# A fused attention, expert and feed-forward kernel: the low halves of expert weights made by an adding DMA instead of GpSimd, and score products over all 128 rows

## The chip, the cores and the metric

The kernel runs on one core of a Trainium2 chip. The metric is the device time of one execution in microseconds (us), the median of three runs. The engines are TensorE (PE; PEld is its weight load), VectorE (DVE), ScalarE (ACT), GpSimd (POOL) and SyncE (SP, which here only issues DMAs).

## The reference

Three blocks follow each other. Only the shapes and the arithmetic matter:

```python
# attention: B, H, S, D = 4, 8, 576, 64
scores = np.where(causal, -1e9, q @ k.T / sqrt(D)); a = exp(scores - max); a /= a.sum(-1) + 1e-9
local = a @ v
mem_out = (phi(q) @ M_prev) / (phi(q) @ z_prev + 1e-6)          # phi(x) = elu(x) + 1
x = g * mem_out + (1 - g) * local                               # g = sigmoid(beta), per head
# experts: N, D, E, F = 2304, 512, 8, 1024; capacity N // E = 288
logits = x @ w_gate        # all (token, expert) pairs by falling logit; a pair is taken
                           # if the token is free and the expert has room
out[mask_e] = maximum(x[mask_e] @ w1[e], 0) @ w2[e]
# second network: d_ff = 2048, w_in and w_out arrive as float64
h = x @ w_in; g = h * tanh(softplus(h)); return g @ w_out
```

## The kernel before, in words

**Precision.** Every fp32 product that counts is made of three fp32r products. A number is held as a high part (rounded to fp32r) and a low part, low = x - high, and the sum takes high x high, low x high and high x low. `mm3` (L998) does this for the networks.

**Attention** has 16 units (a batch and a pair of heads), each in six steps of 128 or 64 query rows: step 4 once for each head ((4,0) and (4,1)), then 2, 1, 0 and 3. A step passes four stages. `stage_a` (L277) makes the scores in PSUM: L298 multiplies 128 rows that hold the high and low q of a head (64 + 64), L304 the low part of k with the high q, 64 rows, one head in the upper and the other in the lower half of the array, and L309 adds the causal mask as a matmul. `stage_b` (L332) transposes the probabilities, `stage_c` (L351 to L359) multiplies them with v and phi(q) with the memory, `stage_d` (L382) finishes. SP loads each unit's q and k, splits them into `q1`, `k1` and `kl` by SBUF transfers (q<-qh, q<-ql, k<-kh), and then issues the loads of the next unit (`ahead`). The last step of the list uses forms of 64 rows or columns where only 64 queries remain.

**The converter** (L745) turns the float64 weights of the second network into fp32 bit by bit on VectorE, with a ScalarE step and, on GpSimd, a product (L783) and a sum (L785). 16 conversions run beside the attention; 16 more are started by `conversions()` (L1088) once four experts are known.

**Experts.** The router works out one expert's tokens after another by a search in thresholds (`phase` L566, `search` L686): VectorE compares (L695, L702), TensorE counts (L707, L722), and they alternate. Each expert has 288 tokens, fetched by three indirect DMAs from GpSimd's queue (L973), transposed on TensorE (L984) and split. Its weights come as 16 tiles `raw` of 128x512 fp32 (L913, on SP; four buffers); for each, ScalarE rounds the high part (L932) and GpSimd subtracts (L942) for the low part, into one of seven `wf` buffers. Once all routing is done VectorE subtracts instead. The second network's first half (resident wa, wb) is woven into the experts, with its gate on ScalarE and VectorE (L1065 to L1081); its second half comes after the experts.

**What sets the order.** TensorE's and GpSimd's orders are written out by a hand planner that hands out slots of six matmuls to generators (`spawn`, `until`); a GpSimd instruction keeps the place it was given. VectorE, ScalarE and SP are ordered by the scheduler from the same program. The dictionary `X` (L1224) holds the planner's settings: LD is the lead, in slots, between a weight's load and its split, RAWB, WFB and ACTB are buffer counts.

Of the kernel before, what the change touches and what calls it, by code (L numbers as in the profile page):

```python
# [33 lines left out]
def attention(tc, ctx, q, k, v, M_prev, z_prev, beta, w_gate, xd, L, side=None):  # L34
# [68 lines left out]

    VZ = []
# [62 lines left out]
    def prep(u, piece):  # L167
# [22 lines left out]
        else:  # L190
# [15 lines left out]
            else:  # L206
# [5 lines left out]
                p["last"] = dq.dma_start(q1[bb, 1], f(p["qh"][bb]))  # L212
# [11 lines left out]
    def prep_first():  # L224
# [26 lines left out]
        for h, s in enumerate(halves):  # L251
# [5 lines left out]
            nc.scalar.copy(r(q1[:, h, 64:S]), tq[h])  # L257
            nc.vector.tensor_sub(r(q1[o, h, 0:64]), zq[o, h], q1[o, h, 0:64])
# [18 lines left out]
    def stage_a(u, i):  # L277
# [17 lines left out]
        kb = (SK - w, 0)  # L295
        for h in heads:
            for a, e in cuts:
                nc.tensor.matmul(vw[h][0:n, a:e], q1[:, h, c0:w], k1[:, h, kb[h] + a:kb[h] + e], start=True,  # L298
                                 stop=False, skip_group_check=True)

        for a, e in cuts:
            for h in heads:
                s = halves[h]
                nc.tensor.matmul(vw[h][0:n, a:e], q1[s, h, c0:w], p["kl"][s, kb[h] + a:kb[h] + e], start=False,  # L304
                                 stop=True, skip_group_check=True)
        for h in heads:

            dg = w - n if h else 0
            nc.tensor.matmul(vw[h][0:n, dg:dg + n], identb[0:n, 0:n], cmask[0:n, 0:n], start=False, stop=True,  # L309
                             skip_group_check=True)  # L310
        if hs is None:
            nc.vector.tensor_reduce(nm[0:n, :], sb[0:n, :, 0:w], axis=AX.X, op=OP.max, negate=True)
        else:
            nc.vector.tensor_reduce(nm[0:n, hs:hs + 1], vw[hs][0:n, 0:w], axis=AX.X, op=OP.max, negate=True)  # L314
        for h in heads:
            nc.scalar.activation(P[0:n, h * w:(h + 1) * w], vw[h][0:n, 0:w], AF.Exp, bias=nm[0:n, h:h + 1], scale=1.0,  # L316
                                 accum_out=den[0:n, h:h + 1])
# [3 lines left out]
    def stage_b(u, i):  # L321
# [7 lines left out]
        for m, eng in GROUPS[i if hs is None else (i, hs)]:  # L329
            t = bank("pt", "pt", 2)  # L330
            for j in range(m):
                nc.tensor.transpose(t[:, j * 128:j * 128 + n], P[0:n, (c + j) * 128:(c + j + 1) * 128],  # L332
                                    ident[0:n, 0:n])
            (nc.scalar.copy if eng else nc.vector.tensor_copy)(  # L334
                T[:, c:c + m, 0:n], t[:, 0:m * 128].rearrange("p (a b) -> p a b", b=128)[:, :, 0:n])
            c += m

    def stage_c(u, i):
# [11 lines left out]
        om = o[0:n, 128 + 2 * W:130 + 4 * W]  # L350
        nc.tensor.matmul(om, p["phi"][:, c0:w], MZ[b % 2][:, hp], start=True,  # L351
# [3 lines left out]
        nc.tensor.matmul(o[:, 0:n], ZB[b]["v"][:, hp, :], T[:, i, 0:n], start=True, stop=(i == 0),  # L355
# [6 lines left out]
        (nc.scalar.copy if i in OTA else nc.vector.tensor_copy)(st["oT"][:, 0:n], o[:, 0:n])  # L362
        nc.vector.tensor_scalar(den[0:n, 2:4], om[:, 2 * W:], 1e-6, None, op0=OP.add)
# [3 lines left out]
    def stage_d(u, i):  # L367
# [14 lines left out]
        nc.tensor.matmul(o[0:n, 128:128 + 2 * W], st["oT"][:, 0:n], R[:, hp].rearrange("p h w -> p (h w)"), start=True,  # L382
# [362 lines left out]
def converter(tc, w_in, w_out):  # L745
# [7 lines left out]
    def convert(a, f, cv, raw, parts=None):  # L753
# [44 lines left out]
def moe(tc, ctx, C, xd, L, w1, w2, w32, whl, convert, out):  # L798
# [19 lines left out]
    eng = [nc.gpsimd, nc.vector]  # L818
# [104 lines left out]

    def splits():
        for c, n, key in order:
# [38 lines left out]
    turned = [-1]  # L964
    xts = {}

    def tokens(k):

        while R.done <= k or turned[0] < k - 1:
# [315 lines left out]
```

## Time and profile before

| | us |
|---|---|
| median of 3 runs (lowest to highest) | 1160.05 (1156.46 to 1165.70) |
| the profiled execution | 1158.69 |
| its span, first to last instruction | 1156.9 |
| mean granted TensorE clock | 0.943 |
| TensorE busy | 1031.9 (89%) |
| VectorE busy | 718.1 (62%) |
| ScalarE busy | 635.5 (55%) |
| GpSimd busy | 407.1 (35%) |

In time the program has a start of some 20 us, the attention to about 300 us, a short stretch in which only the first routing runs (to about 340 us), the experts with the routing of the next ones beside them (to about 820 us), and then the last experts and the second network without routing. A clock of 1.00 is 2.4 GHz; 0.50 is 1.2 GHz, and numbers between them are means over time at both. Most rows below give a start or a stretch in us from the first instruction. An instruction's duration in the trace includes the time in which it has begun and is held up by something that the trace doesn't name.

### The profile page before, as it was taken

The page shows a single profiled execution, that of the slowest core. Times are in us where ns is not written, and L with a number is a line of the kernel's source. Part 1 is how long each engine was busy: PE and PEld are TensorE (multiplying, and loading weights), DVE is VectorE, ACT ScalarE, POOL GpSimd, SP SyncE. Part 2 cuts the span into 40 slices and gives each one's busy share as a digit, 9 for nine tenths or more (in the row PEclk, how much of TensorE's full clock was granted, in tenths as well). Part 3 has the DMA queues.
Part 4 walks back from the last instruction along what each step waited for, and adds up shares of the span by engine and source line. Part 5 has one row for each costly group of instructions (what it writes and reads, how often), then busy time and mean ns, then how long its engine had stood idle before and what let it go on. Part 6 is the DMA issues. An engine that isn't in the chain of part 4 may idle for free.

```text
span 1156.9 us, 22179 instructions
## 1 busy us (share of the span) xinstructions
PE 1031.9 (89%) x8088; PEld 928.7 (80%) x8088; DVE 718.1 (62%) x1954; ACT 635.5 (55%) x1539; POOL 407.1 (35%) x466
## 2 busy tenths in 40 slices
PE   5999999999826969788988879899999999999996
PEld 4777777777625968777877768798999999999996
DVE  7788787865565566658676777768544453333442
ACT  5676676766403443433533443545765786667773
POOL 4676575653207144315325345523200001111112
PEclk9999999999957979889889989989999999999999
DMA  7799689663195232303514422527362532222201
GB/s 179 196 228 234 179 210 230 180 176 82 42 345 149 82 90 91 121 20 107 168 53 134 142 76 96 179 68 248 123 221 75 191 126 83 83 82 83 73 21 41
DMA packets 165628, 153.46 MB, mean 133 GB/s; under 512 B 88912, under 2 KB 134000, under 8 KB 163472
## 3 DMA queue, kind: packets, MB, share of 16 engines
q1 hardware_dynamic: 162272, 142.45, 42.7%
q0 software_dynamic: 3248, 9.61, 2.9%
q8 instruction: 63, 1.03, 0.4%
q14 instruction: 45, 0.37, 0.1%
HBM read 97.17 MB, written 36.18 MB: 115 GB/s over the span
## 4 chain that ended last, share of the span: by engine, by line
PE 67%; DVE 17%; ACT 7%; DMA 4%; issue 2%; POOL 2%; SPq 0%; POOLq 0%; ACTq 0%; DVEq 0%
PE h L1000 20%; PE acc L1000 19%; PE o L359 4%; PE pt L332 4%; PE s L298 3%; PE s L304 3%; PE o L351 2%; PE o L382 2%; DVE H L1078 2%; PE rt L707 2%; DVE cm L702 2%; PE o L355 2%; PE s L309 1%; ACT L1074 1%; PE tr L195 1%
## 5 line engine op out<-in xcount | busy, mean ns | idle before, releaser
L1000 PE MATMUL acc<-act,wb 128*128 128x288 f32 x1536 | 235.5, 304 | 6.2 <-DVE act L1081 2.6
L1000 PEld LDWEIGHTS acc<-act,wb 128*128 128x128 f32 x1536 | 216.8, 193 | 9.1 <-DVE act L1081 3.8
L942 POOL TENSOR_TENSOR wf<-raw,wf 128x512 fp32r<-128x512 f32 x93 | 128.3, 1393 | 239.3 <-ACT wf L932 192.4
L1078 DVE TENSOR_TENSOR H<-H,U 128x288 f32<-128x288 f32 x128 | 68.7, 547 | 177.6 <-ACT U L1074 177.6
L1000 PE MATMUL h<-xt,wf 128*128 128x288 f32 x768 | 126.9, 313 | 3.8 <-DVE xt L993 2.8
L1166 POOL DMA_INDIRECT out<-xg,idx x24 | 25.9, 1077 | 288.3 <-ACT xg L1163 287.0
L1000 PE MATMUL h<-y,wa 128*128 128x288 f32 x768 | 119.7, 311 | 3.4 <-DVE y L993 2.5
L1000 PEld LDWEIGHTS h<-xt,wf 128*128 128x128 f32 x768 | 112.7, 200 | 11.0 <-issue 8.8
L1000 PE MATMUL acc<-act,wf 128*128 128x288 f32 x768 | 120.1, 307 | 0.0
L1000 PEld LDWEIGHTS h<-y,wa 128*128 128x128 f32 x768 | 110.5, 199 | 6.6 <-DVE y L993 3.0
L1000 PE MATMUL h<-xt,wa 128*128 128x288 f32 x768 | 113.2, 296 | 0.0
L932 ACT CAST wf<-raw 128x512 fp32r<-128x512 f32 x128 | 78.8, 617 | 62.1 <-PE acc L1000 20.6
L1000 PEld LDWEIGHTS acc<-act,wf 128*128 128x128 f32 x768 | 108.5, 194 | 4.8 <-issue 4.3
L1000 PEld LDWEIGHTS h<-xt,wa 128*128 128x128 f32 x768 | 105.2, 188 | 0.0
L1065 ACT ACTIVATE U<-h 128x288 f32<-128x288 f32 x128 | 53.2, 416 | 93.0 <-PE h L1000 92.6
L1041 ACT ACTIVATE act<-h 128x288 fp32r<-128x288 f32 x64 | 26.2, 410 | 136.9 <-PE h L1000 136.8
L334 ACT COPY T<-pt 128x512 f32<-128x512 f32 (+4 forms) x128 | 56.8, 446 | 78.7 <-PE pt L332 78.5
L316 ACT ACTIVATE P<-s,nm 128x576 f32<-128x576 f32 (+4 forms) x160 | 83.7, 531 | 6.5 <-DVE nm L314 4.5
L332 PE MATMUL pt<-ident,P 128*128 128x128 f32 (+1 forms) x400 | 68.8, 280 | 0.0
L388 POOL TENSOR_TENSOR xa<-y 128x144 f32<-128x144 f32 (+1 forms) x80 | 47.9, 599 | 44.4 <-DVE y L386 24.2
L707 PEld LDWEIGHTS <-cm 128*32 128x32 bf16 (+1 forms) x756 | 26.2, 107 | 43.7 <-DVE cm L702 30.2
L359 PE MATMUL o<-T,vm 128*64 128x128 f32 x640 | 60.9, 287 | 0.0
(230 smaller groups left out, 2026.8 us busy)
## 6 DMA issues: line engine op xcount, KB each, us to landing
raw<-moe_w SPq DMA_DIRECT2D x128, 256.0 KB, 3.0
k<-kh SPq DMA_DIRECT2D x60, 160.0 KB, 2.9
yd<-y SPq DMA_DIRECT2D x8, 1152.0 KB, 5.3
xt<-yd SPq DMA_DIRECT2D x8, 1152.0 KB, 5.9
raw<-moe_w_in SPq DMA_DIRECT2D x16, 512.0 KB, 4.6
raw<-moe_w_out SPq DMA_DIRECT2D x16, 512.0 KB, 4.5
whl<-parts SPq DMA_DIRECT2D x16, 512.0 KB, 4.5
part<-o SPq DMA_DIRECT2D x8, 576.0 KB, 3.4
```

Source lines behind the costliest of these rows:

```text
L298: nc.tensor.matmul(vw[h][0:n, a:e], q1[:, h, c0:w], k1[:, h, kb[h] + a:kb[h] + e], start=True, stop=False, skip_group_check=True)
L316: nc.scalar.activation(P[0:n, h * w:(h + 1) * w], vw[h][0:n, 0:w], AF.Exp, bias=nm[0:n, h:h + 1], scale=1.0, accum_out=den[0:n, h:h + 1])
L332: nc.tensor.transpose(t[:, j * 128:j * 128 + n], P[0:n, (c + j) * 128:(c + j + 1) * 128], ident[0:n, 0:n])
L334: (nc.scalar.copy if eng else nc.vector.tensor_copy)(T[:, c:c + m, 0:n], t[:, 0:m * 128].rearrange("p (a b) -> p a b", b=128)[:, :, 0:n])
L359: nc.tensor.matmul(o[s, 0:n], vm[:, j - 1 if h else 4 - j, h, :], T[:, i + j if h else i - j, 0:n], start=False, stop=(j == i), skip_group ...
L388: nc.gpsimd.tensor_add(xa[d0:d0 + n, 2 * hp:2 * hp + 2, :], y[0:n, 0:2], y[0:n, 2:4])
L707: nc.tensor.matmul(p[0:T, 0:E], cm[:, j, :], oh[:, j, :], start=(j == 0), stop=(j == NJ - 1))
L932: nc.scalar.copy(dst[:, 0], t)
L942: eng[e].tensor_sub(dst[:, 1], t, dst[:, 0])
L1000: nc.tensor.matmul(p, w[:, a, c * 128:(c + 1) * 128], x(b), start=first and i == 0, stop=last and i == 2)
L1065: s = nc.scalar.activation(U, p[:, 0:CAP], AF.Sigmoid, scale=-1.0)
L1078: nc.vector.tensor_mul(H, H, U)
```

## The change

In the attention two tiles `QZ` of 128 x 2 x 576 are filled with zeros by GpSimd at the start. Each unit writes the high q of its two heads into the upper half of one plane and the lower half of the other, by two further transfers; the other halves stay zero. L304's low product then runs over all 128 rows, as L298 does, and the two heads no longer alternate. Where a step has 64 queries, its matmuls, copies and activations now take all 128 rows or columns.

In the experts, while the routing is not done, ScalarE writes -high into the low part's place with a second activation, and GpSimd issues a DMA that adds `raw` onto it: low = raw - high. GpSimd has no arithmetic left there: the conversions' product and sum go to VectorE. A token's fetch for the first expert may come before any low part (`turned`). LD goes from 10 to 6, RAWB from 4 to 5, ACTB from 13 to 12, and settings without use are dropped.

```diff
+    QZ = []
+    for c in range(2):
+        QZ.append(cp.tile([128, 2, S], F32, name=f"qz{c}"))
+        nc.gpsimd.memset(QZ[c], 0.0)
...
-                p["last"] = dq.dma_start(q1[bb, 1], f(p["qh"][bb]))
+                dq.dma_start(q1[bb, 1], f(p["qh"][bb]))
+                dq.dma_start(QZ[u % 2][a, 0], f(p["qh"][a]))
+                p["last"] = dq.dma_start(QZ[u % 2][bb, 1], f(p["qh"][bb]))
...
+            nc.sync.dma_start(QZ[0][s, h], q1[s, h])
...
+        qz = QZ[u % 2].bitcast(F32R)
+
+        r = slice(c0, c0 + 128)
         for h in heads:
             for a, e in cuts:
-                nc.tensor.matmul(vw[h][0:n, a:e], q1[:, h, c0:w], k1[:, h, kb[h] + a:kb[h] + e], start=True,
+                nc.tensor.matmul(vw[h][:, a:e], q1[:, h, r], k1[:, h, kb[h] + a:kb[h] + e], start=True,
                                  stop=False, skip_group_check=True)
 
-        for a, e in cuts:
-            for h in heads:
-                s = halves[h]
-                nc.tensor.matmul(vw[h][0:n, a:e], q1[s, h, c0:w], p["kl"][s, kb[h] + a:kb[h] + e], start=False,
+            for a, e in cuts:
+                nc.tensor.matmul(vw[h][:, a:e], qz[:, h, r], p["kl"][:, kb[h] + a:kb[h] + e], start=False,
                                  stop=True, skip_group_check=True)
...
-        nc.tensor.matmul(o[:, 0:n], ZB[b]["v"][:, hp, :], T[:, i, 0:n], start=True, stop=(i == 0),
+        nc.tensor.matmul(o[:, 0:128], ZB[b]["v"][:, hp, :], T[:, i], start=True, stop=(i == 0),
...
-    def convert(a, f, cv, raw, parts=None):
+    def convert(a, f, cv, raw, parts=None, eng=nc.gpsimd):
...
-        nc.gpsimd.tensor_mul(r, r, e.bitcast(BF))
+        eng.tensor_mul(r, r, e.bitcast(BF))
         yield
-        nc.gpsimd.tensor_add(r, r, t.bitcast(F32))
+        eng.tensor_add(r, r, t.bitcast(F32))
...
             with tc.high_priority(offset=-400):
                 nc.scalar.copy(dst[:, 0], t)
-            yield 1
-            if c == "wf" and n < X["NV"]:
-                while not R.done:
+                if R.done < E:
+                    nc.scalar.activation(dst[:, 1], t, AF.Copy, scale=-1.0)
+            yield 1
+            if R.done < E:
+
+                while turned[0] < -1:
                     yield 1
-                with R.after():
-                    nc.vector.tensor_sub(dst[:, 1], t, dst[:, 0])
+                nc.gpsimd.dma_start(dst[:, 1].bitcast(F32), t, accum_op=OP.add)
             else:
 
-                e = X["E" + c] if R.done < E else X["EL"] if c == "wf" else X["EB"]
-                eng[e].tensor_sub(dst[:, 1], t, dst[:, 0])
+                nc.vector.tensor_sub(dst[:, 1], t, dst[:, 0])
...
-        while R.done <= k or turned[0] < k - 1:
+        while R.done <= k or turned[0] < min(k - 1, 9 * k - 2):
             yield 1
...
+        turned[0] = max(turned[0], -1)
...
-                yield from convert(a, f, cv, fp.tile([128, 512, 2], I32, name="raw64"))
+                yield from convert(a, f, cv, fp.tile([128, 512, 2], I32, name="raw64"), eng=nc.vector)
```

How the order moves, in three places. First TensorE in the attention's first unit, the score stage with 192 columns (`s` is the score bank, `k_` and `q_` the tiles k1 and q1, `qz_` a QZ tile); before:

```order
L298 MATMUL s<-k_182,q_181 128x192 x2
L304 MATMUL s<-kl,q_181 128x192 x2
L309 LDWEIGHTS identb
L309 MATMUL s<-cmask,identb 128x128
L309 LDWEIGHTS identb
L309 MATMUL s<-cmask,identb 128x128
```

and now:

```order
L309 MATMUL s<-k_186,q_185 128x192
L313 MATMUL s<-kl,qz_150 128x192
L309 MATMUL s<-k_186,q_185 128x192
L313 MATMUL s<-kl,qz_150 128x192
L318 LDWEIGHTS identb
L318 MATMUL s<-cmask,identb 128x128
L318 LDWEIGHTS identb
L318 MATMUL s<-cmask,identb 128x128
```

The heads' low products come right behind their own high products, and all matmuls of the stage have the full array's shape. Then GpSimd, from the end of the attention through the first experts; before:

```order
L942 TENSOR_TENSOR wf<-raw,wf 128x512 x2
L973 DMA xg<-xd,idx 96x512 x3
L942 TENSOR_TENSOR wf<-raw,wf 128x512 x16
L973 DMA xg<-xd,idx 96x512 x3
L942 TENSOR_TENSOR wf<-raw,wf 128x512 x16
L973 DMA xg<-xd,idx 96x512 x3
L942 TENSOR_TENSOR wf<-raw,wf 128x512 x11
L783 TENSOR_TENSOR cvr<-cvr,cve 128x512
L942 TENSOR_TENSOR wf<-raw,wf 128x512
L785 TENSOR_TENSOR cvr<-cvr,cvt 128x512
```

and now:

```order
L982 DMA xg<-xd,idx 96x512 x3
L949 DMA wf<-raw 128x512 x20
L982 DMA xg<-xd,idx 96x512 x3
L949 DMA wf<-raw 128x512 x16
L982 DMA xg<-xd,idx 96x512 x3
L949 DMA wf<-raw 128x512 x10
```

The first fetch of tokens is no longer behind two subtractions, each subtraction is an issue, and the conversions' L783 and L785 are gone from this queue. Last VectorE, behind the first expert's token list (`idx`), in the search for the second expert (`cvt`, `cve`, `cvr` are the converter's tiles); before:

```order
L573 TENSOR_REDUCE m<-L 128x18
L778 SCALAR_TENSOR_TENSOR cvt<-raw_7302,cvt 128x512
L576 TENSOR_TENSOR w<-L,m 128x144
L578 TENSOR_TENSOR mu<-m,pen 128x18
L781 TENSOR_SCALAR cve<-cvt 128x512
L580 TENSOR_TENSOR w<-w,pref 128x144
L702 TENSOR_TENSOR cm<-mu,thi_86 128x576 x2
L582 TENSOR_REDUCE mx<-w 128x18
L584 TENSOR_TENSOR oh<-w,mx 128x144
L993 TENSOR_TENSOR xt<-h,xt 128x288 x4
L1043 SCALAR_TENSOR_TENSOR act<-h,act 128x288 x2
L717 TENSOR_TENSOR ge<-rt,crow 64x8
```

and now:

```order
L710 TENSOR_TENSOR cm<-mu,thi_86 128x576 x2
L791 TENSOR_TENSOR cvr<-cvr,cve 128x512
L590 TENSOR_REDUCE mx<-w 128x18
L793 TENSOR_TENSOR cvr<-cvr,cvt 128x512
L592 TENSOR_TENSOR oh<-w,mx 128x144
L779 TENSOR_SCALAR cvt<-raw_7729 128x512
L782 TENSOR_SCALAR cvt<-cvt 128x512
L785 TENSOR_SCALAR cvt<-cvt 128x512
L786 SCALAR_TENSOR_TENSOR cvt<-raw_7729,cvt 128x512
L1003 TENSOR_TENSOR xt<-h,xt 128x288 x2
L789 TENSOR_SCALAR cve<-cvt 128x512
L1003 TENSOR_TENSOR xt<-h,xt 128x288
```

The product and the sum of a conversion stand between the routing's instructions, and the next conversion (`raw_7729`) follows at once, ahead of the first expert's token split (L1003).

## Rows read from the trace of the kernel before

**Rows 1.** The page, parts 1 and 2: busy us, share, instructions; granted clock in 40 slices.

```profile
PE 1031.9 (89%) x8088; PEld 928.7 (80%) x8088; DVE 718.1 (62%) x1954; ACT 635.5 (55%) x1539; POOL 407.1 (35%) x466
...
PEclk9999999999957979889889989989999999999999
```

**Rows 2.** Stretches: start:end, length; busy PE, PEld, DVE, ACT, POOL; clock, DMA share, GB/s.

```profile
60.00:300.00 240.00, 239.33 (x1896) 180.36 (x1895) 183.06 (x485) 163.49 (x500) 143.64 (x198) 1.00 0.71 180
100.00:200.00 100.00, 99.67 (x799) 75.56 (x798) 78.88 (x207) 67.75 (x210) 65.37 (x87) 1.00 0.85 215
350.00:800.00 450.00, 378.22 (x3064) 354.43 (x3065) 308.12 (x832) 191.46 (x412) 182.84 (x139) 0.90 0.36 111
820.00:1150.00 330.00, 325.78 (x2449) 324.29 (x2448) 133.57 (x349) 218.98 (x467) 32.06 (x51) 1.00 0.31 99
```

**Rows 3.** Waits of TensorE, 340 to 820 us: total, times, longest.

```profile
PE rt L707 <- DVE cm L702: 16.9, 13, 7.8
...
PE h L984 <- POOL wf L942: 11.0, 1, 11.0
```

**Rows 4.** Timeline: start, duration, engine, line, count, idle before; 346 to 350 us.

```profile
346.25 2.94 POOL L942 TENSOR_TENSOR wf<-raw,wf 128x512 fp32r<-128x512 f32 x2 [30.73 <-DVE cvt L777]
...
346.41 1.66 DVE L778 SCALAR_TENSOR_TENSOR cvt<-raw,cvt 128x512 int32<-128x512 int32 x1
...
347.99 1.36 DVE L576 TENSOR_TENSOR w<-L,m 128x144 f32<-128x144 f32 x1
...
349.36 1.06 POOL L973 DMA_INDIRECT xg<-xd,idx  x1 [0.16 <-DVE w L576]
```

**Rows 5.** Chain that ended last: start, duration, what; 400 to 700 us.

```profile
474.44 5.69 DVE oh L584
...
489.30 0.88 DVE H L1078 x2
...
541.46 5.67 DVE cvt L777
```

**Rows 6.** Instructions by line, VectorE; first 340 to 820 us, then 820 to 1150.

```profile
L1078 DVE TENSOR_TENSOR H<-H,U 128x288 f32<-128x288 f32 x44 | 31.1, 721 | 29.4 <-ACT U L1074 29.4
...
L1078 DVE TENSOR_TENSOR H<-H,U 128x288 f32<-128x288 f32 x84 | 37.5, 456 | 148.2 <-ACT U L1074 148.2
...
L942 DVE TENSOR_TENSOR wf<-raw,wf 128x512 fp32r<-128x512 f32 x21 | 14.5, 692 | 6.6 <-ACT wf L932 6.2
```

**Rows 7.** Timeline of TensorE, one score stage and the instruction behind it.

```profile
208.12 0.56 PE L298 MATMUL s<-k,q 128*128 128x320 f32 x2
208.61 0.42 PE L304 MATMUL s<-kl,q 64*128 64x320 f32 x2
208.96 0.28 PE L309 MATMUL s<-cmask,identb 128*128 128x128 bf16 x2
209.08 0.46 PE L382 MATMUL o<-R,oT 128*128 128x144 f32 x2
```

**Rows 8.** Chain, 820 to 860 us: a run of matmuls in one shape.

```profile
820.14 1.59 PE h L1000 x12
```

**Rows 9.** The page, part 6: transfers by issue, size, time to landing (and the DMA view).

```profile
raw<-moe_w SPq DMA_DIRECT2D x128, 256.0 KB, 3.0
...
raw<-moe_w_in SPq DMA_DIRECT2D x16, 512.0 KB, 4.6
...
q<-qh SPq DMA_DIRECT2D x30, 144.0 KB, 2.8
...
wa<-whl SPq DMA_DIRECT2D x8, 512.0 KB, 10.0
```

**Rows 10.** The page, part 5: groups of instructions.

```profile
L942 POOL TENSOR_TENSOR wf<-raw,wf 128x512 fp32r<-128x512 f32 x93 | 128.3, 1393 | 239.3 <-ACT wf L932 192.4
...
L932 ACT CAST wf<-raw 128x512 fp32r<-128x512 f32 x128 | 78.8, 617 | 62.1 <-PE acc L1000 20.6
```

More of the change, by code (lines that the diff above doesn't have):

```diff
@@ L308, in stage_a @@
             dg = w - n if h else 0
-            nc.tensor.matmul(vw[h][0:n, dg:dg + n], identb[0:n, 0:n], cmask[0:n, 0:n], start=False, stop=True,
+            nc.tensor.matmul(vw[h][:, dg:dg + n], identb, cmask[:, 0:n], start=False, stop=True,
                              skip_group_check=True)
         if hs is None:
-            nc.vector.tensor_reduce(nm[0:n, :], sb[0:n, :, 0:w], axis=AX.X, op=OP.max, negate=True)
+            nc.vector.tensor_reduce(nm, sb[:, :, 0:w], axis=AX.X, op=OP.max, negate=True)
         else:
-            nc.vector.tensor_reduce(nm[0:n, hs:hs + 1], vw[hs][0:n, 0:w], axis=AX.X, op=OP.max, negate=True)
+            nc.vector.tensor_reduce(nm[:, hs:hs + 1], vw[hs][:, 0:w], axis=AX.X, op=OP.max, negate=True)
         for h in heads:
-            nc.scalar.activation(P[0:n, h * w:(h + 1) * w], vw[h][0:n, 0:w], AF.Exp, bias=nm[0:n, h:h + 1], scale=1.0,
-                                 accum_out=den[0:n, h:h + 1])
+            nc.scalar.activation(P[:, h * w:(h + 1) * w], vw[h][:, 0:w], AF.Exp, bias=nm[:, h:h + 1], scale=1.0,
+                                 accum_out=den[:, h:h + 1])
         if hs != 0:
@@ L331, in stage_b @@
             for j in range(m):
[L332 to L333 removed]
+                nc.tensor.transpose(t[:, j * 128:(j + 1) * 128], P[:, (c + j) * 128:(c + j + 1) * 128], ident)
             (nc.scalar.copy if eng else nc.vector.tensor_copy)(
[L335 removed]
+                T[:, c:c + m], t[:, 0:m * 128].rearrange("p (a b) -> p a b", b=128))
             c += m
@@ L348, in stage_c @@
         o = st["o"] = bank("o", "o", 2)
-        om = o[0:n, 128 + 2 * W:130 + 4 * W]
-        nc.tensor.matmul(om, p["phi"][:, c0:w], MZ[b % 2][:, hp], start=True,
+        om = o[:, 128 + 2 * W:130 + 4 * W]
+        nc.tensor.matmul(om, p["phi"][:, c0:c0 + 128], MZ[b % 2][:, hp], start=True,
                          stop=True, skip_group_check=True)
         vm = lds[u]["v"]
-        nc.tensor.matmul(o[:, 0:n], ZB[b]["v"][:, hp, :], T[:, i, 0:n], start=True, stop=(i == 0),
+        nc.tensor.matmul(o[:, 0:128], ZB[b]["v"][:, hp, :], T[:, i], start=True, stop=(i == 0),
                          skip_group_check=True)
@@ L361, in stage_c @@
         st["oT"] = wk.tile([128, 128], F32, name="oT", bufs=3)
-        (nc.scalar.copy if i in OTA else nc.vector.tensor_copy)(st["oT"][:, 0:n], o[:, 0:n])
-        nc.vector.tensor_scalar(den[0:n, 2:4], om[:, 2 * W:], 1e-6, None, op0=OP.add)
+        (nc.scalar.copy if i in OTA else nc.vector.tensor_copy)(st["oT"], o[:, 0:128])
+        nc.vector.tensor_scalar(den[0:n, 2:4], om[0:n, 2 * W:], 1e-6, None, op0=OP.add)
     XA = {}
@@ L381, in stage_d @@
         xa = XA[b, i]
-        nc.tensor.matmul(o[0:n, 128:128 + 2 * W], st["oT"][:, 0:n], R[:, hp].rearrange("p h w -> p (h w)"), start=True,
+        nc.tensor.matmul(o[:, 128:128 + 2 * W], st["oT"], R[:, hp].rearrange("p h w -> p (h w)"), start=True,
                          stop=True, skip_group_check=True)
@@ L817, in moe @@
     nc.vector.memset(half_pi, math.pi / 2)
-    eng = [nc.gpsimd, nc.vector]
     ET = mybir.EngineType
@@ L922, in ticking @@
             yield 1
+    turned = [-2]
     def splits():
@@ L1221, in moe @@
     until(lambda: len(scat) == G * E)
-X = {"MO": ("PE", "Pool"), "P": 4, "P0": 4, "L1": 2, "RX": 0, "XB": 2, "LAG": 6, "TW": 18, "TS": 2, "LD": 10,
-     "LG": 2, "RAWB": 4, "WFB": 7, "ACTB": 13, "GB": 7, "NG": 4, "CL": (0, 1.5, 1, 2, 3, 4), "C0": 4,
-     "CW": 8, "FW": 3, "FE": 4, "Ewf": 0, "Ewa": 0, "Ewb": 0, "NV": 0, "AH": 2, "EL": 1,
-     "EB": 1}
+X = {"MO": ("PE", "Pool"), "P": 4, "P0": 4, "L1": 2, "RX": 0, "XB": 2, "LAG": 6, "TW": 18, "TS": 2, "LD": 6,
+     "LG": 2, "RAWB": 5, "WFB": 7, "ACTB": 12, "GB": 7, "NG": 4, "CL": (0, 1.5, 1, 2, 3, 4), "C0": 4,
+     "CW": 8, "FW": 3, "FE": 4, "AH": 2}
 def program(tc, q, k, v, M_prev, z_prev, beta, w_gate, w1, w2, w_in, w_out, out):
```

1 line of the change is left out of this document (removed).

## The prediction

> **What bounds the kernel now.** I read the busy shares and the slices first, then sums over four stretches, then the order of events inside the two stretches that the change touches. TensorE is busy for 89% of the span, and its granted clock falls below nine tenths only in slices 12 to 27 [rows 1]. The stretches say where the missing 11% is [rows 2]. From 60 to 300 us (attention) TensorE is busy 239.33 of 240 us at a clock of 1.00, and from 820 to 1150 us (the last experts and the second network) 325.78 of 330 us at 1.00. Neither has idle time to give; only fewer or shorter matmuls would shorten them. From 350 to 800 us (experts with the routing beside them) it is busy 378.22 of 450 us at a mean clock of 0.90. So 72 us are idle there. A mean of 0.90 between 2.4 and 1.2 GHz is a fifth of the time, 90 us, at the low level; work done in it would take half as long at the high one, which is up to 45 us more. The middle stretch holds between 72 and 117 us, and most of what the change can win.
>
> Who causes the idle time? TensorE waits for VectorE: the largest item is the routing's rt L707 behind cm L702, while the low part of a weight (POOL wf L942) ends a wait of PE only once, for 11 us [rows 3]. VectorE is late because its instructions stretch while GpSimd subtracts: L778 takes 1.66 us and L576 1.36 us beside two L942 that start at 346.25 [rows 4], single instructions on the chain (oh L584, cvt L777) last 5.7 us where a pair of the gate's L1078 takes 0.88 us when nothing is beside it [rows 5], and L1078 averages 721 ns here against 456 ns after 820 us, when GpSimd has no subtractions left [rows 6].
>
> **Attention, part by part.** The low product becomes 128 rows deep, so the stage no longer changes the array's shape between L298, L304 and L309, and the 64-row forms of the last step go. Counted along TensorE's order, neighbours of different shape fall from 501 to 241 with the same number of matmuls. The price of one: a stage with 320 columns takes from 208.12 to 209.08, 0.96 us [rows 7]. In one shape, 12 matmuls of 288 columns take 1.59 us, 133 ns each, 0.46 ns a column [rows 8], which makes 4x320 and 2x128 columns 0.71 us. The 0.25 us left are its two changes, 0.125 us each; 260 of them are 32 us. Some of that is kept by the wider forms of the last step, so I take 1.4 us a unit, 22 us over 16 units, as what TensorE can save.
>
> It can't have all of it. From 100 to 200 us the transfers fill 0.85 of the DMA engines' time at 215 GB/s [rows 2], 253 GB/s when all are busy. The zero-padded q adds two transfers of 64x576 fp32 a unit, 0.29 MB, 1.2 us. At about 18.7 us a unit the engines then need 15.9 + 1.2 = 17.1 us, and TensorE 17.3 us: both near one bound. VectorE's 79 of 100 us [rows 2] are 14.8 us a unit, not the bound. I take two thirds, **-15 us** (0 if the transfers bind, -23 if they don't).
>
> In that stage two 64-row low products of 320 columns take 0.35 us [rows 7], no less than the 0.30 us of two full-row ones at the pitch above.
> The Trainium skill speaks against this half: TensorEngine Tiling (Array Packing), Theoretical Speedup, promises up to twice the throughput for two tiles of 64 rows side by side, which the change would give up. By it the low products of a unit, some 3,200 columns at 0.46 ns, would take half of their 1.48 us before; 0.74 us of the 1.4 would go, and -15 would be -11. The stage above doesn't bear it out, so I leave the sum alone.
>
> At the start, the first low product waits for a transfer that wasn't there: q<-qh lands 2.8 us after its issue [rows 9]; TensorE has nothing else then: **+2 us** (1 to 3). The two fills by GpSimd lie in the loading time: nothing. The next unit's loads on SP now stand behind a transfer that waits for the last reader of the padded tile two units back; loads run a unit ahead, so nothing, and a few us a unit if that lead is gone.
>
> **Experts, part by part.** Removed: 93 subtractions on GpSimd, 128.3 us [rows 10], and 16 pairs of its conversion products. Added: 93 ScalarE activations at the CAST's 617 ns [rows 10], 57 us. ScalarE is busy 191 of 450 us [rows 2], so it goes to 55%: covered, except that a gate's activation can stand 0.6 us longer behind one. Added: 93 DMA issues by GpSimd, about 1.06 us as for a gather [rows 4], 99 us in place of 128. Their landing is in no row; the nearest are 2.8 us for 144 KB and 10.0 us for wa<-whl, 512 KB, the slowest [rows 9]. An add of 256 KB reads both operands; I take 5 us, and 2.8 to 10 for the range. Against the 1.39 us of a subtraction the low part is 5 us later, and since PE waited for it once in the whole stretch and seven weight buffers stand ahead, that costs nothing; at 10 us one more such wait, up to 11 us. Transfers use 0.36 of the engines [rows 2]; 93 adds at some 1.6 us (256 KB written, as much read) are 0.3 more, still under one.
>
> Moved: at the stretch's start the first gathers stand behind two subtractions, 346.25 to 349.36 [rows 4]; now ahead of them: **-3 us**. Moved to VectorE: 16 multiplications and 16 additions of 128x512, at the 0.69 us of its own subtraction [rows 6], 22 us. In VectorE's order all 16 conversions come in the first two experts, between routing instructions, so a late input (4.6 us for a load of 512 KB [rows 9]) would hold the routing behind it. There I give back **+8 us** (0, if they fit into waiting time, to 25, all of it and one load).
>
> Won: VectorE stops stretching. Of 72 idle us I take 40 as gone, since TensorE and VectorE still answer each other in turns in the search; of the 45 us of clock a third, 15, as low stretches follow idle ones: **-55 us** (-20 to -90). Sum of the experts: -3 + 8 - 55 = -50. Retuned lead and buffer counts: nothing, since the loads land in 3.0 us [rows 9] and no wait of PE names one; if a lead of six slots were too short, a load's 3.0 us would show now and then. After 820 us nothing changes.
>
> Total -15 + 2 - 50 = -63. The profiled execution took 1158.69 us (span 1156.9), 1.4 below the median of the runs, so the forecast is 1158.7 - 63 = 1096, stated as **1097 us** against the median.
>
> **Rivals.**
> - *The adds become the bound (slower).* A raw buffer is held through load 3.0, two activations 1.2, issue 1.1 and landing. With five buffers, 93 weights in the 474 us that they now span allow 5.1 us each, 25 us a buffer: the point is a landing of 20 us. At 23 us it is 5.7 us each, 530 us: +56 - 13 = 1202 us. For it: every add is issued in order on one queue, whose head waits for ScalarE; against: the slowest row is 10 us.
>  The Trainium skill has a way to it: SBUF - State Buffer, the "DVE blocks DMA" trap, says that descriptors of GpSimd's transfers can't be written while VectorE holds the ports that both share; no run so far shows it for an add, and a gather beside a busy VectorE issued in 1.06 us [rows 4]. I give it 0.03 of this rival's chance, at the same 1202 us, since GpSimd's queue would then be the slow part of the cycle.
> - *Conversions bind VectorE.* Experts 0 and 1 then run at VectorE's pace and a load's delay, and the win is only in the later ones: 1097 + 30 = 1127 us. For it: the order's crowding; against: VectorE is at 68% [rows 2], stretching included.
> - *Attention gains nothing*, transfers bind it: 1111 us.
> - *The idle time stays.* If the search's turns, not stretched instructions, make TensorE wait, or the adds stretch VectorE as subtractions do, only attention wins and the conversions cost: about 1150 us. For it: several waits end on very short instructions; against: the 5.7 us ones on the chain.
>
> **How the numbers follow.** Forecast 0.47 (its own range 1072 to 1112), conversions bind 0.16, attention nothing 0.08, idle time stays 0.14 (half of it within 1%), adds bind 0.13, better than 1072 0.02. Runs of this kernel tell about 1%, 11.6 us, apart. Faster: 0.47 + 0.16 + 0.08 + 0.07 + 0.02 = 0.80; within 1%: 0.07; slower: 0.13. Above 1150 lie the 0.13 and a little of the idle time that stays; the low end takes in three quarters of what the middle stretch can win: 1063 to 1150.
>
> **What would show it.** Right: in the attention stretch the unit's pitch falls by 0.9 us with TensorE still full; L1078 near 460 ns and no single VectorE instruction over 2 us between 350 and 800; clock above 0.95 there; adds landing in 3 to 8 us with PE not waiting for wf. Wrong: PE or ScalarE (a full set of raw buffers) waiting for adds; VectorE waiting for raw loads of conversions with routing behind; the attention's DMA share at 0.95 and more with PE idle.

## The result, and the profile after

The changed kernel takes 1129.09 us (median of 6 runs, 1126.80 to 1135.30) against 1156.51 us before in the same sessions; the ratio is 0.9754, with a 95% interval of 0.9718 to 0.9789. It is faster by some 28 us. The forecast was a gain of 63 us, to 1097 us: the direction was right and the time lies inside the range of 1063 to 1150, but less than half of the gain came. The profiled execution took 1130.89 us (span 1129.1).

The page of the changed kernel, parts 1, 2 and 5, in answer to [rows 1, 6, 10]:

```profile
PE 1011.6 (90%) x8088; PEld 935.1 (83%) x8088; DVE 651.4 (58%) x1986; ACT 680.8 (60%) x1632; POOL 325.8 (29%) x436
...
PEclk9999999999956888988989999999999999999998
...
L949 POOL DMA_DIRECT2D wf<-raw x93 | 81.3, 939 | 271.6 <-ACT wf L943 162.1
L1088 DVE TENSOR_TENSOR H<-H,U 128x288 f32<-128x288 f32 x128 | 57.0, 455 | 177.2 <-ACT U L1084 177.1
...
L941 ACT CAST wf<-raw 128x512 fp32r<-128x512 f32 x128 | 78.9, 616 | 72.9 <-DMA raw<-moe_w 53.4
```

VectorE's total fell from 718 to 651 us although it was given 32 further instructions of some 0.69 us: the stretching is gone. The gate's product (L1088, L1078 before) takes 455 ns in the mean. The last of these lines holds what has grown: ScalarE's casts wait 53.4 us for loads of weights to land. Before, from 340 to 820 us, it was

```profile
ACT wf L932 <- DMA raw<-moe_w: 17.6, 10, 5.9
```

(total, times, longest, in us).

The same stretches as [rows 2], of the changed kernel:

```profile
60.00:300.00 240.00, 233.90 (x1993) 195.34 (x1994) 180.21 (x503) 168.45 (x521) 147.20 (x206) 1.00 0.79 199
100.00:200.00 100.00, 96.34 (x826) 80.44 (x825) 81.23 (x214) 70.23 (x220) 64.05 (x87) 1.00 0.92 222
350.00:800.00 450.00, 395.90 (x3218) 372.40 (x3218) 261.73 (x893) 257.94 (x546) 103.93 (x110) 0.92 0.68 172
```

TensorE still idles 54 us between 350 and 800 and the clock rose only from 0.90 to 0.92. The DMA share there went from 0.36 to 0.68, as forecast. Cut at 500 us, the middle shows where the gain went. Before:

```profile
350.00:500.00 150.00, 124.26 (x1031) 114.55 (x1032) 91.97 (x268) 62.66 (x135) 59.59 (x46) 0.89 0.35 103
500.00:800.00 300.00, 253.97 (x2034) 239.88 (x2034) 216.16 (x564) 128.80 (x277) 123.25 (x93) 0.91 0.37 114
```

and changed:

```profile
350.00:500.00 150.00, 117.50 (x868) 107.65 (x868) 101.12 (x320) 74.01 (x151) 38.45 (x40) 0.83 0.83 212
500.00:800.00 300.00, 278.40 (x2352) 264.75 (x2352) 160.60 (x573) 183.93 (x396) 65.48 (x71) 0.96 0.61 152
```

From 500 us on TensorE is fuller by 24 us and its clock is 0.96. In the first 150 us, experts 0 and 1, it does less than before: 868 matmuls for 1031, at a clock of 0.83. By the first product of each expert in the timeline, experts 0 and 1 take 177.1 us where they took 149.0, and experts 2 to 6 292.1 where they took 334.8. A gain of 42.7 us stands against a loss of 28.1. The attention ends 11.6 us earlier (its last product with the memory starts at 300.7, before at 312.3).

### The profile page after: what moved, and what is told of

The parts are those of the page before. It is cut to its first block, busy times and chain, and to the rows that moved or that the text cites. A ratio compares the mean times of both kernels' runs of the same rounds, so it can differ in the third digit from the quotient of the medians.

```text
span 1129.1 us, 22472 instructions
## 1 busy us (share of the span) xinstructions
PE 1011.6 (90%) x8088; PEld 935.1 (83%) x8088; DVE 651.4 (58%) x1986; ACT 680.8 (60%) x1632; POOL 325.8 (29%) x436
## 3 DMA queue, kind: packets, MB, share of 16 engines
q0 software_dynamic: 16640, 33.99, 15.7%
## 4 chain that ended last, share of the span: by engine, by line
PE 41%; DMA 7%; ACT 6%; DVE 5%; issue 2%; POOL 0%; POOLq 0%; SPq 0%; ACTq 0%; DVEq 0%
PE h L1010 20%; PE acc L1010 19%; DMA wf<-raw 2%; DMA raw<-moe_w 2%; DMA w<-cvr 1%; ACT L1084 1%; DVE H L1088 1%; PE rt L715 1%; ACT U L1084 1%; DMA raw<-moe_w_in 1%; PE h L1171 1%; ACT U L1075 1%; DVE act L1091 1%; PE h L994 0%; ACT U L1080 0%
## 5 line engine op out<-in xcount | busy, mean ns | idle before, releaser
L1010 PEld LDWEIGHTS acc<-act,wb 128*128 128x128 f32 x1536 | 214.4, 191 | 9.6 <-DVE act L1090 3.3
L949 POOL DMA_DIRECT2D wf<-raw x93 | 81.3, 939 | 271.6 <-ACT wf L943 162.1
L1088 DVE TENSOR_TENSOR H<-H,U 128x288 f32<-128x288 f32 x128 | 57.0, 455 | 177.2 <-ACT U L1084 177.1
L941 ACT CAST wf<-raw 128x512 fp32r<-128x512 f32 x128 | 78.9, 616 | 72.9 <-DMA raw<-moe_w 53.4
L342 ACT COPY T<-pt 128x512 f32<-128x512 f32 (+3 forms) x128 | 57.5, 456 | 59.1 <-PE pt L341 58.8
L341 PE MATMUL pt<-ident,P 128*128 128x128 f32 x400 | 69.8, 282 | 1.1 <-DVE T L342 0.9
L367 PE MATMUL o<-T,vm 128*64 128x128 f32 x640 | 64.2, 288 | 0.0
L780 ACT ACTIVATE cvr<-raw 128x512 f32<-128x512 uint16 x32 | 21.8, 681 | 65.2 <-DMA raw<-moe_w 34.7
L309 PE MATMUL s<-k,q 128*128 128x288 f32 (+3 forms) x192 | 59.6, 347 | 1.4 <-ACT P L325 0.7
```

The lines of the kernel that those rows point to most:

```text
L309: nc.tensor.matmul(vw[h][:, a:e], q1[:, h, r], k1[:, h, kb[h] + a:kb[h] + e], start=True, stop=False, skip_group_check=True)
L341: nc.tensor.transpose(t[:, j * 128:(j + 1) * 128], P[:, (c + j) * 128:(c + j + 1) * 128], ident)
L342: (nc.scalar.copy if eng else nc.vector.tensor_copy)(T[:, c:c + m], t[:, 0:m * 128].rearrange("p (a b) -> p a b", b=128))
L367: nc.tensor.matmul(o[s, 0:n], vm[:, j - 1 if h else 4 - j, h, :], T[:, i + j if h else i - j, 0:n], start=False, stop=(j == i), skip_group ...
L949: nc.gpsimd.dma_start(dst[:, 1].bitcast(F32), t, accum_op=OP.add)
L1010: nc.tensor.matmul(p, w[:, a, c * 128:(c + 1) * 128], x(b), start=first and i == 0, stop=last and i == 2)
```

## The experiments

Times are medians of the runs of that kernel, ratios are to the kernel before, timed beside it. The changed kernel's own ratio is 0.9754.

**The two parts alone** (e1: attention as changed, all else as before; e2: the reverse).

> The attention part alone (zero-padded q, full-row products), experts as before. All theories: the attention ends 11 to 12 us earlier, as in the changed kernel's profile, and nothing else moves: 1156.5 - 12 = 1144.5 us (1141 to 1148). If part of the earlier end came from something in the experts' code, less: 1150 us or more.

> The experts' part alone (adding DMA, conversions on VectorE, lead and buffers), attention as before. If the parts add: 1156.5 - 15 = 1141 us (1138 to 1145), and with the attention part they make the 27 us of the whole. If they hinder each other (experts 0 and 1 starved by an earlier start), less: 1135 us or lower.

Measured: e1 1148.39 us, 0.9915 (0.9884 to 0.9947), a gain of 10 us; e2 1137.48 us, 0.9822 (0.9770 to 0.9873), a gain of 21 us. They add up to the whole within their intervals. The attention gave a little less than expected and the experts a little more; most of what the forecast misses is in the experts (21 us for 50).

**The attention's transfers** (e12, on e1):

```diff
-                dq.dma_start(QZ[u % 2][a, 0], f(p["qh"][a]))
-                p["last"] = dq.dma_start(QZ[u % 2][bb, 1], f(p["qh"][bb]))
...
-            nc.sync.dma_start(QZ[0][s, h], q1[s, h])
```

> The attention part alone without its two further transfers a unit: the padded q stays zero, so the low product of k with the high q is left out of the scores. Experts as before. It tells what the transfers cost in the attention, where the DMA share is 0.80 and 0.95 in its densest stretch. If the transfers bind the attention: 1148 - 7 = 1141 us (1137 to 1144), and no unit longer than 18 us. If VectorE binds the units in which a batch starts (20 to 24 us there, 15 to 17 elsewhere): 1146 to 1149 us, those units as long.

Measured: 1143.43 us, 0.9849 (0.9797 to 0.9901), against e1's 0.9915. The time lies in the first expectation's range, but the intervals overlap, so the times alone don't settle it. The traces say more. From 80 to 140 us, in the kernel before, e1 and e12:

```profile
80.00:140.00 60.00, 59.67 (x477) 45.23 (x478) 50.08 (x129) 41.56 (x128) 39.54 (x54) 1.00 0.85 210
...
80.00:140.00 60.00, 56.99 (x474) 48.06 (x473) 48.42 (x129) 42.42 (x128) 40.92 (x54) 0.97 0.95 231
...
80.00:140.00 60.00, 59.38 (x515) 49.74 (x513) 51.66 (x137) 43.57 (x137) 42.31 (x56) 1.00 0.86 224
```

With the two further transfers the DMA share is 0.95 and TensorE idles 3 us of 60; without them it is 0.86 and 0.6 us. By the first score product of each unit, the three long units in the attention behind the first two (the third, seventh and eleventh) take 19.2, 22.5 and 19.0 us in e1 and 19.8, 17.8 and 17.8 in e12 (19.0, 19.4 and 19.4 before the change): the transfers make the last two longer, and the first is long without them. The attention's last product with the memory starts at 297.6 us in e12 and at 303.5 in e1. That is 6 us in one trace of each.

**Where the conversions lie** (e3; e4 puts their product and sum back on GpSimd instead, `eng=nc.vector` left out).

```diff
-                nc.sync.dma_start(raw.bitcast(U16).rearrange("p f w -> p (f w)"),
+                lq.dma_start(raw.bitcast(U16).rearrange("p f w -> p (f w)"),
...
-                yield from convert(a, f, cv, fp.tile([128, 512, 2], I32, name="raw64"), eng=nc.vector)
+                yield from convert(a, f, cv, fp.tile([128, 512, 2], I32, name="raw64"), eng=nc.vector, lq=nc.gpsimd)
```

> The changed kernel, with the loads of the 16 late conversions issued from GpSimd's queue in place of SP's. That queue is in the planner's order, so the conversions lie as far apart as in the kernel before (1, 2, 2, 3 in experts 2 to 5 and 8 behind) instead of 8 and 8 in experts 0 and 1; VectorE's work, ScalarE's and the bytes stay the same. Theory 1 (bunched conversions hold VectorE and ScalarE behind their loads and stores): experts 0 and 1, now 88 and 89 us, return to 60 to 75: 1129 - 28 = 1101 us (1093 to 1110). Theory 2 (the transfers bind: DMA share 0.84 in experts 0 and 1): the adds and loads of weights remain, only 8 of 30 MB leave that stretch: 1119 to 1125 us. Theory 3 (22 us more work on VectorE): the work only moves: 1124 to 1130 us.

> The changed kernel, with the conversions' product and sum back on GpSimd; the adding DMA stays. The planner's order spreads the conversions here too. Theory 1: experts 0 and 1 return to 60 to 75 us, and 32 GpSimd products of 1.3 us stretch VectorE again in the later experts, 10 us or so: 1105 to 1115 us. Theory 2: 1119 to 1125 us. Theory 3 (VectorE's added work): all 22 us come back where VectorE is late: 1105 to 1110 us; so this run tells theories 1 and 3 from 2, and the pinned loads tell 1 from 3.

Measured: e3 1126.80 us, 0.9719 (0.9670 to 0.9769); e4 1130.70 us, 0.9751 (0.9702 to 0.9800). Neither differs from the changed kernel. Theory 1's 1101 us is refuted for the total, e4 refutes theory 3 as well (1105 to 1110), and neither median falls in theory 2's range. e4 is also the price of that whole move, order and stretching included: with the conversions' product and sum back on GpSimd nothing is won or lost, within some 7 us. What theory 1 says of experts 0 and 1 is there all the same, as the two stretches of e3 show:

```profile
350.00:500.00 150.00, 134.36 (x1154) 123.24 (x1153) 79.21 (x299) 85.58 (x182) 37.65 (x43) 0.93 0.68 160
500.00:800.00 300.00, 260.21 (x2106) 247.81 (x2105) 189.11 (x608) 172.22 (x367) 75.61 (x84) 0.94 0.70 179
```

With the conversions out of experts 0 and 1, TensorE is busy 134 of 150 us there, and 18 us less later. The loss moved with the conversions.

**The adds.** A new look at the changed kernel's chain, past expert 1, showed what no theory had yet named (start, duration, what):

```profile
547.81 4.10 DMA wf<-raw
...
552.02 4.74 DMA raw<-moe_w
...
557.39 0.62 ACT wf L943
...
561.50 7.07 DMA wf<-raw
...
568.67 2.65 DMA raw<-moe_w
...
571.33 0.46 DVE y L1003
```

An add lands, which frees a raw buffer; SP issues the next load into it; ScalarE stands at the cast until it lands; then the next add. It is a ring of five buffers, and the other work of ScalarE and VectorE stands in order behind it. SP's queue shows how close together the weights come here:

```profile
549.67 19.35 SPq L920 DMA_DIRECT2D raw<-moe_w  x9
```

Nine loads in 19 us start 2.4 us apart, where the 93 adds of the whole kernel are 4.4 us apart in the mean (341.7 to 751.1 us). From 546 to 572 us the DMA engines are full besides: their share is 1.0, where it is 0.68 from 350 to 800. The waits of the whole changed kernel (total, times, longest), SyncE's queue and ScalarE:

```profile
SPq L920 <- DMA wf<-raw: 256.6, 79, 20.8
...
ACT wf L941 <- DMA raw<-moe_w: 53.4, 26, 6.5
```

Four runs test it. e5 only drops the add's line; e6 also drops the second activation and subtracts on VectorE instead, as in the diff; e7 the same with `nc.gpsimd.tensor_sub`; e8 is the change in the last two lines alone. e5's results, like those of e12 above and e13 below, are not the reference's.

```diff
-                if R.done < E:
-                    nc.scalar.activation(dst[:, 1], t, AF.Copy, scale=-1.0)
...
-                nc.gpsimd.dma_start(dst[:, 1].bitcast(F32), t, accum_op=OP.add)
+                nc.vector.tensor_sub(dst[:, 1], t, dst[:, 0])
```

```diff
-     "LG": 2, "RAWB": 5, "WFB": 7, "ACTB": 12,
+     "LG": 2, "RAWB": 8, "WFB": 7, "ACTB": 9,
```

> The changed kernel with its 93 adding DMAs left out: the low part stays at minus the high part, so the products are not the reference's. ScalarE's two activations, the conversions and all else stay. Theory 4 (since the adds, a raw buffer is held through load, activations and an add's landing; ScalarE stands in order behind loads that wait for a buffer, and the gate behind ScalarE): 42 us of the chain in 350 to 800 are adds and the loads behind them, so 1129 - 30 = 1099 us (1090 to 1108). Theory 5 (the search's turns between VectorE and TensorE set the pace, and the adds fill what is left): 1121 to 1129 us.

> The changed kernel with the low part by a VectorE subtraction in place of the second activation and the adding DMA; GpSimd still has no arithmetic in the experts. VectorE gets 93 x 0.69 = 64 us more, ScalarE 57 us less, the DMA engines 24 MB less, and a raw buffer is free at once. Theory 4: the ring's 30 us come back and some of VectorE's 64 are lost: 1110 to 1135 us. Theory 5 (VectorE and the search set the pace): most of the 64 us is added: 1150 to 1185 us.

> The changed kernel with the low part by GpSimd's subtraction as before; conversions stay on VectorE, attention and buffers as changed. This is the price of the adding DMA alone against GpSimd's arithmetic. If the stretching of VectorE was what the change took away: 93 subtractions return it, 1150 us (1143 to 1158). If the adding DMA costs about as much as the stretching: 1125 to 1135 us.

> The changed kernel with eight raw buffers in place of five, paid for with nine activation buffers in place of twelve. Theory 4: loads run ahead of the adds' landing and ScalarE no longer stands behind them: 1129 - 20 = 1109 us (1102 to 1116), with ScalarE's waits for loads of weights, 53 us before, under 20. Theory 5, or if nine activation buffers bind: 1124 us or more.

Measured: e5 1107.67 us, 0.9557 (0.9531 to 0.9582); e6 1120.27 us, 0.9662 (0.9631 to 0.9693); e7 1146.89 us, 0.9894 (0.9865 to 0.9924); e8 1113.89 us, 0.9621 (0.9586 to 0.9655). e5, e6 and e8 fall where theory 4 put them and outside theory 5's; e7 falls where the stretching put it. So the adds cost some 22 us by being there (0.9754 to 0.9557), and three more buffers win back 15 of them. Against GpSimd's subtraction the adding DMA wins 16 us; against VectorE's it loses 10, as long as it has five buffers. In e8 the same two waits, and in e6, with five buffers and no adds, ScalarE's, are

```profile
SPq L920 <- DMA wf<-raw: 187.0, 60, 17.5
...
ACT wf L941 <- DMA raw<-moe_w: 15.1, 8, 5.6
...
ACT wf L941 <- DMA raw<-moe_w: 10.1, 11, 3.2
```

SP still waits for adds in e8, but ScalarE, which matters, waits little for its loads. e6 bears on the objection that five buffers are too few for any kernel: without adds ScalarE hardly waits for its loads with five either. Its time with eight was not run.

**Both remedies together** (e9: e8 with e3's loads; e10: e6 with them; e11: e9 with VectorE's subtraction for every second weight).

> Eight raw buffers (nine activation buffers) and the late conversions' loads on GpSimd's queue together. The pinned loads alone made experts 0 and 1 36 us shorter and the later ones 31 us longer. Theory 4: the later ones grew because a conversion delays ScalarE and with it a ring of five buffers; with eight the loss goes: 1114 - 15 = 1099 us (1090 to 1106). Theory 1b: a conversion costs the same some 2 us wherever it stands between the routing's instructions: 1110 to 1116 us.

> VectorE subtracts (no second activation, no adding DMA) and the late conversions' loads stand on GpSimd's queue. There is no ring through an add here, so if theory 4 is right about the pinned run's loss, spreading the conversions gains what it won in experts 0 and 1, less what VectorE lacks later: 1120 - 15 = 1105 us (1098 to 1114). Theory 1b: 1117 to 1122 us.

> As the run with eight raw buffers and pinned loads, but every second low part by a VectorE subtraction: half of the adds and second activations, 46 x 0.69 = 32 us more on VectorE. If eight buffers with 93 adds still hold ScalarE: 4 to 10 us less than that run. If they don't: the same or up to 10 us more, by VectorE's work.

Measured: e9 1114.35 us, 0.9623 (0.9569 to 0.9676); e10 1136.49 us, 0.9811 (0.9754 to 0.9869); e11 1119.97 us, 0.9657 (0.9602 to 0.9712). e9 is the time of e8, as theory 1b has it: with the adds, a conversion costs the same wherever it stands between routing instructions. e10 doesn't fit it: it is slower than e6 by 16 us, against both expectations, and why spreading hurts there, where VectorE also subtracts, stays open. e11 is no better than e9, so with eight buffers half of the adds can go without a gain.

**What a conversion costs** (e13: e8 without the VectorE part of the 16 late conversions; e14: e8 with a lead of ten slots; e15: ten raw and seven activation buffers; e16: e8 with two buffers each for a conversion's input and result, paid for with two activation buffers). The diff is e16's.

```diff
-        r = cv.tile([128, 512], F32, name="cvr")
+        r = cv.tile([128, 512], F32, name="cvr", bufs=2 if parts is None else 1)
...
-                yield from convert(a, f, cv, fp.tile([128, 512, 2], I32, name="raw64"), eng=nc.vector)
+                yield from convert(a, f, cv, fp.tile([128, 512, 2], I32, name="raw64", bufs=2), eng=nc.vector)
...
-     "LG": 2, "RAWB": 5, "WFB": 7, "ACTB": 12,
+     "LG": 2, "RAWB": 8, "WFB": 7, "ACTB": 7,
```

> Eight raw buffers, and the 16 late conversions without their VectorE instructions: load, one ScalarE activation and store stay, so the second network's late weights are not converted rightly. Theory 1c (a conversion's cost is VectorE's work and VectorE's in-order wait for its load, wherever it stands): experts 0 and 1, 90 and 79 us with eight buffers, go to 60 to 68, 1114 - 35 = 1079 us (1070 to 1090). Theory 1d (it is the transfers' share and ScalarE's waits for loads and stores, which stay): 1105 to 1114 us.

> Eight raw buffers with the lead between a load and its split back at 10 slots (6 in the changed kernel). If ScalarE still meets loads that haven't landed (15 us of waits with eight buffers): 1109 us (1104 to 1112). If the later split costs as much as it saves: 1112 to 1118 us.

> Ten raw buffers and seven activation buffers. If the ring still holds at eight: 1108 us (1103 to 1112). If eight were enough, or seven activation buffers hold back the matmuls' next slots: 1112 to 1125 us.

> Eight raw buffers and two buffers each for a late conversion's input and its result (seven activation buffers pay for it). VectorE's work stays, but its in-order wait for a conversion's load (25 us in experts 0 and 1 with eight raw buffers) and ScalarE's for a store (21 us) can be covered by the conversion before. If these waits make the conversions dear: 1114 - 12 = 1102 us (1095 to 1107). If it is VectorE's 63 us of work itself, or seven activation buffers cost what is won: 1106 to 1116 us.

Measured: e13 1096.21 us, 0.9448 (0.9405 to 0.9490); e14 1116.51 us, 0.9646 (0.9598 to 0.9694); e15 1107.53 us, 0.9574 (0.9523 to 0.9625); e16 1100.49 us, 0.9486 (0.9445 to 0.9526). VectorE's part of the conversions costs 20 us with eight buffers (0.9621 to 0.9448): less than theory 1c's 35 and more than theory 1d's 0 to 9, and the time lies in neither range. That is the whole part, most of which VectorE had before the change too, not only the product and the sum that were moved. e16 keeps all that work, has two activation buffers fewer, and gains 16 us: most of the cost goes with the in-order wait for a conversion's load. VectorE's waits in experts 0 and 1 (346 to 530 us), with eight raw buffers (e8):

```profile
DVE cvt L779 <- DMA raw<-moe_w_in: 24.9, 7, 11.1
...
DVE cvt L779 <- DMA raw<-moe_w_out: 1.6, 3, 0.9
```

and with the double buffers (e16):

```profile
DVE cvt L779 <- DMA raw<-moe_w_out: 7.3, 2, 5.5
DVE cvt L779 <- DMA raw<-moe_w_in: 0.9, 1, 0.9
```

26.5 us became 8.2. The second result buffer could have helped as well, but ScalarE's wait for a conversion's store hardly moved in the same stretch (20.6 to 16.3 us). In e6, without adds, VectorE waits only 6.0 us for these loads: most of the wait comes with the adds. The conversions' loads stand in SP's queue among the loads of weights, which wait for adds, and that may be why; no run shows it. The lead of ten slots (e14) changes nothing; ten raw buffers (e15) may be a little better than eight, the intervals overlap. Eleven raw with six activation buffers (e17) gave no time: that program deadlocks.

**Does the add pay, then?** (e18: e6 with double conversion buffers and ACTB 9; e19: e16 with RAWB 10 and WFB 6.)

> VectorE subtracts in place of the adding DMA, and the late conversions have two buffers each (nine activation buffers, five raw ones, which no add holds here). It asks whether the adding DMA pays once nothing waits in order behind it. If VectorE's 64 us of subtractions are the difference that is left: 1100 + 8 = 1108 us (1104 to 1115), slower than the adds with eight raw buffers and the same double buffers. If they are covered: 1096 to 1102 us.

> Ten raw buffers, double buffers for the late conversions, and six buffers for split weights in place of seven. If the ring still holds at eight: 1095 us (1090 to 1098). If six split buffers take the place of the ring: 1101 to 1110 us.

Measured: e18 1116.45 us, 0.9624 (0.9586 to 0.9662); e19 1100.87 us, 0.9492 (0.9454 to 0.9529). With its waits covered the adding DMA (e16) is 16 us better than VectorE's subtraction (e18); five buffers and single ones turned that into a loss of 10. The second conversion buffers bring 16 us beside the adds (e8 to e16) but only 4, inside the intervals, without them (e6 to e18). e19 is e16 again: either the ring no longer holds at eight, or the split buffer that was given up costs what two raw ones bring. **e16 and e19 are the fastest: e16 takes 1100.49 us, 5.1% less than the kernel before and 2.7% less than the changed one** (0.9486 over 0.9754).

## Why the prediction was wrong

The terms of its sum, against the runs:

- *Attention, -15 and +2.* Measured -10 (e1, 6 to 13 by its interval). The saving in TensorE's work was sized about right in sum (the medians of the score stages in the two traces give 1.2 us a unit for 1.4), but not in its parts. The stage with two heads and 320 columns that the prediction priced took 0.96 us [rows 7] and was to fall to 0.71; in e1 it takes 0.80 (153.97 to 154.77), so by the prediction's division a change of shape cost 0.08 us there, not 0.125. The stage with one head and 288 columns, twice a unit, gives more: 1.09 us before (202.30 to 203.39), 0.71 in e1 (200.29 to 201.00). First e1's 320 columns, then 288 columns before and in e1:

```profile
153.97 0.39 PE L309 MATMUL s<-k,q 128*128 128x320 f32 x1
154.20 0.31 PE L313 MATMUL s<-kl,qz 128*128 128x320 f32 x1
154.35 0.31 PE L309 MATMUL s<-k,q 128*128 128x320 f32 x1
154.49 0.31 PE L313 MATMUL s<-kl,qz 128*128 128x320 f32 x1
154.65 0.28 PE L318 MATMUL s<-cmask,identb 128*128 128x128 bf16 x2
154.77 0.61 PE L341 MATMUL pt<-ident,P 128*128 128x128 f32 x4
...
202.30 0.53 PE L298 MATMUL s<-k,q 128*128 128x288 f32 x2
202.76 0.53 PE L304 MATMUL s<-kl,q 64*128 64x288 f32 x2
...
203.39 0.27 PE L332 MATMUL pt<-ident,P 64*128 64x64 f32 x1
...
200.29 0.54 PE L309 MATMUL s<-k,q 128*128 128x288 f32 x2
200.66 0.43 PE L313 MATMUL s<-kl,qz 128*128 128x288 f32 x2
...
201.00 0.28 PE L341 MATMUL pt<-ident,P 128*128 128x128 f32 x1
```

 What limits it was half seen. The forecast took the DMA engines' mean share over 100 us, 0.85 [rows 2]; in the densest 60 us the added transfers bring it to 0.95 and TensorE idles (e1 against e12 above).

 The rule that spoke against this half (the Trainium skill, TensorEngine Tiling (Array Packing), Theoretical Speedup: up to twice the throughput for 64-row tiles side by side) finds no support here: the stage with two heads became shorter, 0.96 to 0.80 us, when its 64-row pairs were given up. The stage with one head says nothing of it, since both of its 64-row products lie in the same half of the array. The measurement decides.

- *VectorE stops stretching, -55.* The mechanism held: L1088 at 455 ns for L1078's 721 [rows 6], and no VectorE instruction between 340 and 820 us longer than 0.77 us, where single ones had lasted 5.7 us [rows 5]. Its size didn't. From e7, which has GpSimd's subtractions, to e5, which has neither them nor adds, the time falls by 39 us, where 55 were forecast. With the adds in their place 16 are left (e7 to the changed kernel). The 42.7 us past the first two experts are not all its work, since conversions also left that stretch. The signs that the prediction named came half: adds land in 5 us, and TensorE doesn't wait for them, but the clock between 350 and 800 us is 0.92, not 0.95. Its three signs of being wrong all came: ScalarE waits behind the adds, VectorE waits for the conversions' loads, and the attention's DMA share reaches 0.95 with TensorE idle.

- *The adds' landing "costs nothing", the step that failed.* The landing was sized well: 4.9 us forecast 5; in the changed kernel's list of issues

```profile
raw<-moe_w SPq DMA_DIRECT2D x128, 256.0 KB, 4.1
wf<-raw POOLq DMA_DIRECT2D x93, 256.0 KB, 4.9
```

 What was asked of it was wrong. The prediction compared the delay with TensorE's need of the low part (once waited for [rows 3], seven buffers ahead), and TensorE indeed hardly waits for it. But the raw buffer is held until the add has landed, the next load (4.1 us now, 3.0 before [rows 9]) starts only then, and ScalarE waits for that load at the head of its queue, with the gate's and the relu's activations behind it. The rival on the adds had this very cycle, but with mean rates: 25 us a buffer would have allowed a landing of 20 us. The weights don't come at a mean rate: loads 2.4 us apart, as shown above, leave each of five buffers 12 us in place of 25, and load, activations, issue and landing take 4.1 + 1.2 + 0.9 + 4.9 = 11.1. There the ring is at its limit. Measured: 22 us (e5), 15 of them given back by three buffers (e8), with the same bytes to move. The DMA engines are full in such a stretch too, where the prediction counted their mean share ("still under one"); whether that makes the other 7 us, no run shows.

- *Conversions on VectorE, +8.* The move itself costs nothing that the runs can tell: e4 takes it back and the time is the same. The prediction saw that "a late input would hold the routing behind it", and such waits are there: 22.9 us in experts 0 and 1 of the changed kernel, and 26.5 in e8. They belong to the instructions that VectorE had before as well, and they are long beside the adds (6.0 us in e6). With eight buffers, covering them wins 16 us (e16).

The terms can be followed through a chain of runs, each step within some 5 us. From e1 (attention alone, 0.9915) to e7 (conversions, earlier first fetch and buffers as changed, GpSimd still subtracting, 0.9894) the time falls by 2 us; from there to e5 (no subtraction, no add, the second activation kept, 0.9557) by 39; from there to the changed kernel (0.9754) it rises by 22. That makes -19 where -50 was forecast. Of the 31 us between them 22 are the adds, which the prediction put at nothing. The rest is what the subtractions' removal won, 39 for 55, less what the smaller terms did better, -2 for +5.

That e16 comes near the forecast of 1097 us doesn't confirm its sum: e16 has buffers that the changed kernel hasn't, and the terms were others. The rival nearest the measured time, conversions that bind VectorE (1127 us), has the picture right, experts 0 and 1 slower and the later ones faster. As a cause it fails: e3 and e4 take the conversions out of experts 0 and 1 and the total stays. That its time agrees is luck.

The "DVE blocks DMA" trap (the Trainium skill, SBUF - State Buffer) leaves no sign here: the adds' issue on GpSimd takes 939 ns in the mean, less than a gather's 1.06 us [rows 4], with VectorE busy 58% of the span.

## What to carry to other kernels

When an operation on an engine becomes a transfer, ask not only who needs its result but what it holds until it lands, here the source buffer, and which in-order queue stands behind the next use of it; count buffers for bursts, not for the mean rate. A wait at the head of an in-order queue can come from another change: a second buffer for the conversions was worth 16 us beside the adds and 4, inside the intervals, without them, so try a remedy in the kernel in which it is to stand. To price a move, take back the move alone (e4), not all the work around it (e13). And a loss that moves when the work is moved (e3) is not yet understood: look for what it waits for in both places.

## What the runs showed of the hardware

An adding DMA from SBUF to SBUF doesn't stretch VectorE: the gate's product takes 455 ns in the changed kernel with its 93 adds, 456 ns in e5, which has neither adds nor subtractions, and 515 ns in e7 between 340 and 820 us, with GpSimd's subtractions. It loads the DMA engines: the changed kernel's software queue holds 15.7% of 16 engines' span, 2.9% before; the difference, 144 us over 93 adds, is 1.5 us each for 256 KB. Loads of weights land in 4.1 us in the median, 3.0 before and in e7, which has as many raw buffers and no adds.

```profile
q0 software_dynamic: 16640, 33.99, 15.7%
```
